# An FFT stage as two 64-row matmuls side by side, whole-row loads from SyncE, and a new order table

## The chip, the cores and the metric

The kernel runs on one core of one Trainium2 chip. The metric is the time of one launch on the device in microseconds (us), as the median of several launches on the same chip. One launch in each measurement is also recorded by the hardware profiler; the profile lines below come from that launch. A profile's span is 1.6 to 2.2 us shorter than the timed launch.

Names of the engines in the lines: PE is TensorE's matmul side, PEld its weight loads, DVE is VectorE, ACT is ScalarE, POOL is GpSimd, SP is SyncE (here it only issues loads and stores); a "q" behind a name (ACTq) is the engine's issuing side. L with a number is a line of the kernel.

## The reference

Four residual layers on x, 2048 x 640: a state-space recurrence A, a long convolution B gated by the normalized x, and both again with the same parameters.

```python
def _A_ref(x, Lambda_re, ..., Dskip):              # cut
    Lam_bar = exp(dt * Lam);  B_bar = ((Lam_bar - 1) / Lam)[:, None] * Bmat
    Bu = einsum("bld,pd->blp", x + 0j, B_bar)
    for t in range(L): h = Lam_bar * h + Bu[:, t]
    return 2 * einsum("blp,dp->bld", hseq, Cmat).real + x * Dskip

def _B_ref(q, k, v, shift_k, ssm_k, ssm_D):        # cut
    kv = causal_shift(k, shift_k) * v              # 4 taps
    y = irfft(rfft(pad(kv)) * rfft(pad(ssm_k)))[:S]
    return q * (y + kv * ssm_D)

x = x + _A_ref(_layernorm(x), ...)
x = x + _B_ref(_layernorm(x), B_k, B_v, ...)
x = x + _A_ref(_layernorm(x), ...)
x = x + _B_ref(_layernorm(x), B_k, B_v, ...)
```

The convolution does not depend on x. The kernel computes it once, in the "FFT part" up to some 160 us, beside the first pieces of layer A; the rest (the projections of the two A layers, chunk by chunk) is dense TensorE work.

## The kernel before

The 4096-point transforms are matmuls with small tables. Channels go through in five groups ("quarters"); each takes stage A (a table FA over 16 x 8 rows), an eviction from PSUM to SBUF, stage B (tables Cf, Sf), another eviction, products of spectra, and the inverse way. Stage A and the eviction helper:

```python
def evac(nc, eng, out, in_):                       # L285: one PSUM tile to SBUF, bf16
    if eng == "act":
        nc.scalar.activation(out, in_, ACT.Copy)
    else:
        nc.vector.tensor_copy(out, in_)

def stage_A(name, s_x, s_A, deps):
    outs = []
    for g in range(NOC // 4):                      # 4 tiles of 1024 f32 columns
        s_ps = R_ps.new()
        def e_m(_, g=g, s_ps=s_ps):
            pa = s_ps.get()[:].rearrange("p (o n) -> p o n", n=256)
            for o4 in range(4):
                nc.tensor.matmul(pa[:, o4, :], lhsT=s_x.get()[:, 4 * g + o4, :], rhs=T["FA"][:], start=True, stop=True)
        t_m = S.add(f"{name}:m{g}", "pe", c_mm(256, 4), deps + TK["fa"], e_m, uses=[s_ps, s_x, s_A])
        def e_e(eng, g=g, s_ps=s_ps):
            pa = ...                               # cut
            evac(nc, eng, vA(s_A.get())[:, :, 32 * g:32 * g + 32]..., pa)
        outs.append(S.add(f"{name}:e{g}", ("act", "dve"), ..., [t_m], e_e, uses=[s_A, s_ps]))
    return outs
```

PSUM is held by one ring of four tiles of 1024 columns, shared by all stages:

```python
"ps": store(psp, 4, "ps", [P, 1024], F32),
R_ps = St["R_ps"] = Ring(St["ps"], 4, lambda t: t[:], in_order=False)
```

Each `S.add` is a task with an engine (or two to choose from), an estimated time and its dependencies. A small scheduler, when the program is built, plays these estimates through and fixes every engine's order; the priorities come from a table of numbers per task name (`WHEN`). The engines then run their instructions strictly in that order. The two matrices B of layer A come in ten loads on ScalarE's queue, 256 B a row:

```python
for k in range(NJ):
    nc.scalar.dma_start(out=B[i][:, k], in_=src[:, k * P:(k + 1) * P].rearrange("(j p) e -> p j e", p=P))
```

The weights W0 and W1 come from C: 20 transposing loads, 20 scalings on ScalarE, 20 products on VectorE (two W per row block).

Of the kernel before, what the change touches and what calls it, by code (L numbers as in the profile page):

```python
# [9 lines left out]
ALU = mybir.AluOpType  # L10
# [7 lines left out]
P = 128  # L18
# [26 lines left out]
NB5 = 13  # L45
QGRP = [(0, 4), (4, 8), (8, 12), (12, 16), (16, 17)]
# [4 lines left out]
    "yt_io0": -271.6, "yt_ph0": 326, "yt_sin0": -120, "yt_neg0": -228.7, "yt_io6": 435.5, "yt_ph6": 22.8, "yt_sin6": -279.2, "yt_neg6": -141, "yt_io12":  # L51
    -220.6, "yt_ph12": -457.1, "yt_sin12": 437.4, "yt_neg12": 474.2, "yt_Ci": -245.6, "yt_Si": -161.3, "yt_nsi": -157.4, "yt_f0": -70.8, "yt_f1": -556.5,
    "yt_f2": -307.9, "yt_f3": -711.6, "yt_f4": 665.9, "kv_dsl": -59.1, "kv_d0": 150.8, "kv_d1": -77.1, "kv_d2": 0.9, "kv_ds0": -18.1, "kv_lk0": 528.3,
    "kv_lv0": 465, "kv_mm0": -259.3, "kv_ev0": -129.3, "kv_st0": -237.4, "kv_ds1": -220.1, "kv_lk1": -362.1, "kv_lv1": 704.6, "kv_mm1": 421.8, "kv_ev1":
    325.4, "kv_st1": 450.7, "kv_ds2": -305.2, "kv_lk2": 82.3, "kv_lv2": 465.6, "kv_mm2": -58.2, "kv_ev2": 145.9, "kv_st2": -165.8, "kv_ds3": 427.5,
    "kv_lk3": 70.5, "kv_lv3": 784.7, "kv_mm3": -40.1, "kv_ev3": 435.7, "kv_st3": -667.8, "kv_ds4": 512.6, "kv_lk4": -76.8, "kv_lv4": 422.1, "kv_mm4":
    -75.5, "kv_ev4": 132, "kv_st4": -45.9, "a_pl": -229.9, "a_p0": -261.5, "a_p1": 363.3, "a_p2": 347.9, "a_p3": -204.3, "a_p4": 255.2, "a_p5": 238,
    "a_p6": -249.8, "a_lamd": -396.5, "a_f": 2, "a_dd": -77.4, "a_ldB0": 23.4, "a_ldB1": -101.3, "a_wl00": -75.8, "a_wc00": -393.6, "a_wm00": -74.3,
    "a_wl01": 413.8, "a_wc01": -46.1, "a_wm01": 462.5, "a_wl02": 405.4, "a_wc02": -8.9, "a_wm02": -423.1, "a_wl03": 602.1, "a_wc03": 474.3, "a_wm03":
    -284.3, "a_wl04": 398.8, "a_wc04": -220.6, "a_wm04": -196.3, "a_wl10": -330.9, "a_wc10": -726.1, "a_wm10": 480.1, "a_wl11": 96.3, "a_wc11": -174.6,  # L60
    "a_wm11": -121.9, "a_wl12": 540.6, "a_wc12": 315.8, "a_wm12": 384.3, "a_wl13": -423.6, "a_wc13": 415, "a_wm13": -86.8, "a_wl14": 94.7, "a_wc14":
    -197.2, "a_wm14": -366.3, "a_b00": 339.9, "a_b0e0": -243.8, "a_b01": -303.4, "a_b0e1": -84.2, "a_b10": 367, "a_b1e0": 297.9, "a_b11": 537.4, "a_b1e1":
    -116.3, "a_gm0": -283, "a_ge0": 230.7, "a_gm1": 391.6, "a_ge1": 422.7, "a_gm2": 365.8, "a_ge2": -84.5, "a_gm3": 457.2, "a_ge3": 101, "a_gm4": 211.1,
    "a_ge4": -226.2, "a_t0": 91, "a_t1": -216.1, "a_t2": -113.7, "yq0_kl": -341.3, "yq0_ka": -222.8, "yq0_KA": 241, "yq0_KB": 409.1, "yq0_vl": -144.2,
    "yq0_VA": 324.9, "yq0_VB": -344, "yq1_kl": 361.5, "yq1_ka": -99.1, "yq1_KA": -347.4, "yq1_KB": -93.8, "yq0_pw": 251.1, "yq0_IB": -230.3, "yq0_tt":
    -225.5, "yq1_vl": 52.6, "yq1_VA": -147.3, "yq1_VB": -360.3, "yq0_IA": -427.3, "yq0_st": -247.4, "yq2_kl": -176.6, "yq2_ka": 326.8, "yq2_KA": -106.6,
    "yq2_KB": -222.6, "yq1_pw": -315.3, "yq1_IB": 346.7, "yq1_tt": -85.5, "yq2_vl": 505.1, "yq2_VA": 425.8, "yq2_VB": -57.5, "yq1_IA": 342.6, "yq1_st":
    -310.8, "yq3_kl": -681.2, "yq3_ka": -307.1, "yq3_KA": -687.6, "yq3_KB": 367.3, "yq2_pw": 540.8, "yq2_IB": -72.6, "yq2_tt": -46.2, "yq3_vl": 303.2,
    "yq3_VA": -299.1, "yq3_VB": -173.9, "yq2_IA": 544.4, "yq2_st": 512.3, "yq4_kl": -221.5, "yq4_ka": 583.5, "yq4_KA": 313.2, "yq4_KB": -706.1, "yq3_pw":
    75, "yq3_IB": -253.9, "yq3_tt": 477.5, "yq4_vl": -383.9, "yq4_VA": -63.8, "yq4_VB": 435.3, "yq3_IA": 285, "yq3_st": -339.1, "yq4_pw": 430.2, "yq4_IB":  # L70
    -600.2, "yq4_tt": -149.8, "yq4_IA": 302.1, "yq4_st": 393.8, "xl0": -445.4, "A1c0_ln_bn": 274, "A1c0_ln_sd": -264.9, "A1c0_ln_post": -71.3, "A1c0_id":
    -56.3, "A1c0_tu": -45.4, "A1c0_bp": 410, "A1c0_ev": -115.6, "A1c0_ri": -445.4, "A1c0_sc": -70.1, "A1c0_cy": -117.7, "A1c0_ro": -414.3, "A1c0_xr": 405,
    "A1c0_cp": -348.8, "A1c0_xe": -161.7, "xl1": 349.4, "A1c1_ln_bn": -263.7, "A1c1_ln_sd": 426.3, "A1c1_ln_post": -182.2, "A1c1_id": -45.6, "A1c1_tu":
    -390.5, "A1c1_bp": 554.8, "A1c1_ev": 433.4, "A1c1_ri": 62.5, "A1c1_sc": -176.6, "A1c1_cy": 692.2, "A1c1_ro": 257.4, "A1c1_xr": -229.1, "A1c1_cp":
    -301.2, "A1c1_xe": -187.2, "xl2": 489.2, "A1c2_ln_bn": 185.5, "A1c2_ln_sd": 42.9, "A1c2_ln_post": -273.1, "A1c2_id": -275.6, "A1c2_tu": 506.7,
    "A1c2_bp": 419.2, "A1c2_ev": -192.7, "A1c2_ri": -352.9, "A1c2_sc": 513.9, "A1c2_cy": 479.9, "A1c2_ro": 47.2, "A1c2_xr": 427.3, "A1c2_cp": 353.2,
    "A1c2_xe": -295.7, "xl3": 473.4, "A1c3_ln_bn": 436.7, "A1c3_ln_sd": -180.6, "A1c3_ln_post": -95.8, "A1c3_id": 501, "A1c3_tu": -171.8, "A1c3_bp":
    -284.2, "A1c3_ev": -23.6, "A1c3_ri": 474.8, "A1c3_sc": 262.9, "A1c3_ro": -55.3, "A1c3_xr": 88.2, "A1c3_cp": -259.4, "A1c3_xe": -282.6, "yl0": -306,
    "B1c0_ln_nm": -98, "B1c0_ln_sq": 59.3, "B1c0_ln_sd": 316, "B1c0_ln_post": 264.9, "B1c0_u": 256.2, "B1c0_m": 580.5, "A2c0_ln_nm": -307.9, "A2c0_ln_sq":
    -182.8, "A2c0_ln_sd": -188.6, "A2c0_ln_post": -48.1, "A2c0_id": 264.9, "A2c0_tu": 351.8, "A2c0_bp": -344.1, "A2c0_ev": -255.5, "A2c0_ri": -339.4,  # L80
    "A2c0_sc": 454.9, "A2c0_cy": 294.9, "A2c0_ro": -132.7, "A2c0_cp": -140.3, "A2c0_xe": 146.6, "yl1": 548, "B1c1_ln_nm": -62.5, "B1c1_ln_sq": 488,
    "B1c1_ln_sd": 544.9, "B1c1_ln_post": -353.5, "B1c1_u": -21.4, "B1c1_m": -58.3, "A2c1_ln_nm": 16.9, "A2c1_ln_sq": 550.5, "A2c1_ln_sd": -350.9,
    "A2c1_ln_post": -111.4, "A2c1_id": -172.3, "A2c1_tu": -255.8, "A2c1_bp": -229.7, "A2c1_ev": -110.4, "A2c1_ri": -95, "A2c1_sc": 249.4, "A2c1_cy":
    -412.5, "A2c1_ro": 473.1, "A2c1_cp": 453.6, "A2c1_xe": -412.8, "yl2": -87.5, "B1c2_ln_nm": 384.2, "B1c2_ln_sq": -409.3, "B1c2_ln_sd": 477.3,
    "B1c2_ln_post": 152.3, "B1c2_u": 497, "B1c2_m": 217.2, "A2c2_ln_nm": 338.6, "A2c2_ln_sq": 536.1, "A2c2_ln_sd": -93.8, "A2c2_ln_post": -401.5,
    "A2c2_id": 276.9, "A2c2_tu": -287.5, "A2c2_bp": -481.5, "A2c2_ev": 390.2, "A2c2_ri": 354.5, "A2c2_sc": -258.3, "A2c2_cy": 318.6, "A2c2_ro": 461.6,
    "A2c2_cp": 663.3, "A2c2_xe": -375.5, "yl3": 106.6, "B1c3_ln_nm": -193.4, "B1c3_ln_sq": 442, "B1c3_ln_sd": -114.2, "B1c3_ln_post": -416, "B1c3_u":
    523.6, "B1c3_m": -137.8, "A2c3_ln_nm": -203.6, "A2c3_ln_sq": 311.2, "A2c3_ln_sd": -189.5, "A2c3_ln_post": 529.5, "A2c3_id": -41.6, "A2c3_tu": -51.1,
    "A2c3_bp": -163.8, "A2c3_ev": -88.5, "A2c3_ri": 467.4, "A2c3_sc": -424.5, "A2c3_ro": 249, "A2c3_cp": 120.6, "A2c3_xe": 3.3, "B2c0_ln_nm": -65.3,
    "B2c0_ln_sq": -228.2, "B2c0_ln_sd": -207.9, "B2c0_ln_post": -254.7, "B2c0_u": -207.5, "B2c0_m": -58.2, "B2c0_st": 220.9, "B2c1_ln_nm": -628.9,  # L90
    "B2c1_ln_sq": -280, "B2c1_ln_sd": -119.4, "B2c1_ln_post": -430.8, "B2c1_u": -47.4, "B2c1_m": -25.8, "B2c1_st": 511.3, "B2c2_ln_nm": 494.3,
    "B2c2_ln_sq": -346.8, "B2c2_ln_sd": -142.4, "B2c2_ln_post": -421.9, "B2c2_u": 480.3, "B2c2_m": 70.7, "B2c2_st": 246.6, "B2c30_ln_nm": -252.7,
    "B2c30_ln_sq": -253.9, "B2c30_ln_sd": -542.9, "B2c30_ln_post": -437, "B2c30_u": -53, "B2c30_m": 535.7, "B2c31_ln_nm": -332.9, "B2c31_ln_sq": 450.9,
    "B2c31_ln_sd": 582.3, "B2c31_ln_post": -162.7, "B2c31_u": 169.1, "B2c31_m": 482.4, "B2c31_st": -150, "B2c32_ln_nm": 242.5, "B2c32_ln_sq": -75.7,
    "B2c32_ln_sd": -334.8, "B2c32_ln_post": -61.5, "B2c32_u": -209.4, "B2c32_m": 425.8, "B2c33_ln_nm": 520, "B2c33_ln_sq": 510.3, "B2c33_ln_sd": -286.2,
    "B2c33_ln_post": 91.1, "B2c33_u": -240.3, "B2c33_m": -214.5, "B2c33_st": -561.6,
}

# [178 lines left out]
def c_act(n):  # L277
    return 0.05 + 0.00083 * n
# [1084 lines left out]
```

## Time and profile before

| | before |
|---|---|
| time, median of 4 launches | 371.06 us (370.37 to 372.15) |
| span of the profile | 368.1 us |
| PE, VectorE, ScalarE busy | 329.2, 316.3, 258.2 us |
| first matmul of stage B | 31.6 us |
| PE idle by columns (prediction's formula): to stage B, middle, tail | 23.5, 14.9, 9.6 us |

Kept apart by shape, an eviction of 1024 columns lasts 1.04 us on ScalarE and 1.22 us on VectorE:

```profile
L287 ACT ACTIVATE b<-ps 128x1024 bf16<-128x1024 f32 x103 | 99.9, 1041 | 13.6 <-PE ps L666 11.0 <-PE ps L1042 1.2 <-PE ps L1069 0.9
...
L289 DVE CAST b<-ps 128x1024 bf16<-128x1024 f32 x18 | 21.7, 1220 | 11.0 <-PE ps L1042 5.8 <-PE ps L1069 5.0 <-PE ps L1146 0.2
```

Stage A makes 1024 columns with four matmuls in 0.44 us. The two longest waits of PE itself between 26 and 160 us in the kernel before (us in total, times, longest) name those evictions:

```profile
PE ps L1064 <- ACT b L287: 3.3, 5, 1.5
PE ps L1042 <- ACT b L287: 1.8, 6, 0.4
```

Here L1042 is stage A, L1064 stage B.

### The profile page before, as it was taken

The page shows a single profiled execution, that of the slowest core. Times are in us where ns is not written, and L with a number is a line of the kernel's source. Part 1 is how long each engine was busy: PE and PEld are TensorE (multiplying, and loading weights), DVE is VectorE, ACT ScalarE, POOL GpSimd, SP SyncE. Part 2 cuts the span into 40 slices and gives each one's busy share as a digit, 9 for nine tenths or more (in the row PEclk, how much of TensorE's full clock was granted, in tenths as well). Part 3 has the DMA queues.
Part 4 walks back from the last instruction along what each step waited for, and adds up shares of the span by engine and source line. Part 5 has one row for each costly group of instructions (what it writes and reads, how often), then busy time and mean ns, then how long its engine had stood idle before and what let it go on. Part 6 is the DMA issues. An engine that isn't in the chain of part 4 may idle for free.

```text
span 368.1 us, 7994 instructions
## 1 busy us (share of the span) xinstructions
PE 329.2 (89%) x3332; PEld 247.8 (67%) x3332; DVE 316.3 (86%) x483; ACT 258.2 (70%) x402; POOL 22.1 (6%) x54
## 2 busy tenths in 40 slices
PE   0259998999998899899999999999999999999990
PEld 0137777877877688788578577577587855865550
DVE  8666579699699799399998999977978999999996
ACT  0397689996879999993158859896677440813893
POOL 6035502000000000000000000000000000000000
PEclk9999999999999999999999999999999999999996
DMA  9983999999999975766044760453014005040042
GB/s 205 199 151 92 212 183 187 228 184 181 253 190 228 177 142 110 112 204 128 0 77 112 154 262 3 99 154 104 2 27 117 3 0 73 2 143 2 36 144 107
DMA packets 124510, 45.88 MB, mean 125 GB/s; under 512 B 118709, under 2 KB 118714, under 8 KB 124474
## 3 DMA queue, kind: packets, MB, share of 16 engines
q1 hardware_dynamic: 115152, 43.20, 53.2%
q10 hardware_dynamic: 9322, 2.18, 3.6%
q8 instruction: 26, 0.43, 0.5%
q14 instruction: 10, 0.08, 0.1%
HBM read 17.38 MB, written 7.86 MB: 69 GB/s over the span
## 4 chain that ended last, share of the span: by engine, by line
PE 70%; ACT 13%; DVE 9%; issue 3%; DMA 2%; POOL 1%; ACTq 1%; DVEq 0%; POOLq 0%
PE ps L752 32%; PE ps L663 10%; PE ps L666 10%; ACT b L287 8%; PE ps L1000 5%; PE ps L512 3%; PE ps L1042 2%; DMA b<-in_B_ssm_k_dram 2%; DVE bs L599 2%; PE ps L1145 1%; PE ps L1146 1%; PE ps L1064 1%; ACT b L458 1%; PE ps L1067 1%; POOL b L392 1%
## 5 line engine op out<-in xcount | busy, mean ns | idle before, releaser
L287 ACT ACTIVATE b<-ps 128x1024 bf16<-128x1024 f32 (+3 forms) x126 | 110.2, 956 | 17.4 <-PE ps L666 14.8
L752 PEld LDWEIGHTS <-b 128*128 128x128 bf16 x880 | 67.7, 98 | 48.3
L752 PE MATMUL ps<-W,b 128*128 128x128 bf16 (+1 forms) x640 | 95.9, 299 | 0.0
L663 PE MATMUL ps<-b,BT 128*128 128x256 bf16 x400 | 56.7, 273 | 0.6 <-ACT b L287 0.5
L666 PE MATMUL ps<-b,BT 128*128 128x256 bf16 x400 | 56.7, 273 | 0.0
L619 ACT ACTIVATE b<-b,nmr,rstd 128x640 bf16<-128x640 f32 (+1 forms) x51 | 44.0, 918 | 7.4 <-DVE nmr L586 7.3
L701 DVE TENSOR_TENSOR_SCAN b<-rtab,b 128x1290 bf16<-128x1290 f32 x16 | 44.6, 2832 | 0.2
L663 PEld LDWEIGHTS <-BT 128*128 128x128 bf16 x400 | 38.7, 98 | 5.2 <-issue 0.9
L666 PEld LDWEIGHTS <-BT 128*128 128x128 bf16 x400 | 39.1, 98 | 4.5
L574 ACT ACTIVATE junk<-b,nmean 128x640 bf16<-128x640 f32 x48 | 39.8, 828 | 1.5
L1064 PE MATMUL ps<-b,b 128*128 128x128 bf16 x170 | 35.1, 219 | 4.0 <-ACT b L287 3.3
L1067 PE MATMUL ps<-b,b 128*128 128x128 bf16 x170 | 35.3, 219 | 0.0
L289 DVE CAST b<-ps 128x1024 bf16<-128x1024 f32 (+1 forms) x23 | 23.5, 1045 | 13.1 <-PE ps L1069 7.1
L1069 PE MATMUL ps<-b,b 128*128 128x128 bf16 x150 | 32.8, 219 | 0.0
L1066 PE MATMUL ps<-b,b 128*128 128x128 bf16 x150 | 32.8, 219 | 0.0
L752 PE MATMUL ps<-G,b 128*128 128x512 bf16 (+1 forms) x160 | 27.0, 299 | 0.0
L760 ACT ACTIVATE b<-ps 128x640 f32<-128x640 f32 x16 | 11.2, 699 | 21.6 <-PE ps L752 21.5
L1042 PE MATMUL ps<-FA,b 128*128 128x256 bf16 x160 | 22.6, 285 | 3.3 <-ACT b L287 1.8
L569 ACT ACTIVATE nmean<-sums 128x4 f32<-128x4 f32 (+1 forms) x15 | 3.0, 203 | 29.0 <-DVE b L764 22.7
L1042 PEld LDWEIGHTS <-b 128*128 128x128 bf16 x160 | 15.8, 102 | 7.9 <-issue 3.9
L1145 PE MATMUL ps<-b,b 128*128 128x128 bf16 x160 | 18.4, 219 | 0.9 <-DVE b L1006 0.9
L1000 PE MATMUL ps<-b,fd 128*128 128x512 bf16 x80 | 18.4, 379 | 0.6 <-ACT b L287 0.6
(207 smaller groups left out, 573.3 us busy)
## 6 DMA issues: line engine op xcount, KB each, us to landing
b<-in_A_x_dram SPq DMA_DIRECT2D x8, 640.0 KB, 5.4
b<-ysd SPq DMA_DIRECT2D x8, 640.0 KB, 4.2
kvd<-b SPq DMA_DIRECT2D x5, 512.0 KB, 3.1
b<-kvd SPq DMA_DIRECT2D x5, 512.0 KB, 4.3
ysd<-b SPq DMA_DIRECT2D x5, 512.0 KB, 4.0
out_dram<-b SPq DMA_DIRECT2D x8, 320.0 KB, 2.2
b<-in_B_ssm_k_dram SPq DMA_DIRECT2D x4, 512.0 KB, 5.8
tab<-in_A_B_im_dram ACTq DMA_DIRECT2D x5, 160.0 KB, 4.2
```

Source lines behind the costliest of these rows:

```text
L287: nc.scalar.activation(out, in_, ACT.Copy)
L574: nc.scalar.activation(small.junk, src(q), ACT.Square, bias=st["nmean"][:, i:i + 1], scale=1.0, accum_out=st["ssq"][:, i:i + 1])
L619: nc.scalar.activation(dst, src, ACT.Identity, bias=st["nmr"][:, i:i + 1], scale=st["rstd"][:, i:i + 1])
L663: nc.tensor.matmul(pb[:, jj, c2, :], lhsT=aw["BT1"][:, c2, j, k, :], rhs=uT[:, k, 0:2, :].rearrange("p t i -> p (t i)"), start=(k == 0), s ...
L666: nc.tensor.matmul(pb[:, jj, c2, :], lhsT=aw["BT0"][:, c2, k, j * P:(j + 1) * P], rhs=uT[:, k, 2:4, :].rearrange("p t i -> p (t i)"), star ...
L701: nc.vector.tensor_tensor_scan(gv, rt, gv, 0.0, ALU.mult, ALU.add)
L752: nc.tensor.matmul(pc[:, o0:o1], lhsT=lh, rhs=rh, start=(n == 0), stop=(n == len(ops) - 1))
L1000: nc.tensor.matmul(pk[:, 512 * b:512 * (b + 1)], lhsT=s_ds.get()[:, l, :], rhs=kT[:, t0:t0 + 512], start=(l == 0), stop=(l == 3))
L1042: nc.tensor.matmul(pa[:, o4, :], lhsT=s_x.get()[:, 4 * g + o4, :], rhs=T["FA"][:], start=True, stop=True)
L1064: nc.tensor.matmul(ps[:, g, 0, :], lhsT=T["Cf"].get()[:, q, :], rhs=are, start=True, stop=single)
L1066: nc.tensor.matmul(ps[:, g, 0, :], lhsT=T["Sf"].get()[:, q, :], rhs=A[:, 2 * q + 1, :], start=False, stop=True)
L1067: nc.tensor.matmul(ps[:, g, 1, :], lhsT=T["NSf"].get()[:, q, :], rhs=are, start=True, stop=single)
```

## The change

The intent is to use the two halves of TensorE's rows at once in stage A, where each output needs only 64 of the 128 rows, and to start earlier. Stage A:

```diff
-            pa = s_ps.get()[:].rearrange("p (o n) -> p o n", n=256)
+            pa = s_ps.get()[:].rearrange("p (h s o e) -> p h o s e", h=2, o=4, e=4)
             for o4 in range(4):
-                nc.tensor.matmul(pa[:, o4, :], lhsT=s_x.get()[:, 4 * g + o4, :], rhs=T["FA"][:], start=True, stop=True)
+                for h in range(2):
+                    hs = slice(64 * h, 64 * (h + 1))
+                    nc.tensor.matmul(pa[:, h, o4, :], lhsT=s_x.get()[hs, 4 * g + o4, :],
+                                     rhs=T["FA"][hs, :].rearrange("p (s e) -> p s e", e=4), start=True, stop=True)
...
-    T["FA"] = wp.tile([P, 256], BF, tag="FA", name="FA")
+    T["FA"] = wp.tile([P, P], BF, tag="FA", name="FA")
```

The loads, in whole rows and on SyncE, and the scheduler's model of the queue:

```diff
-            for k in range(NJ):
-                nc.scalar.dma_start(out=B[i][:, k], in_=src[:, k * P:(k + 1) * P].rearrange("(j p) e -> p j e", p=P))
+            nc.sync.dma_start(out=B[i], in_=src.rearrange("(j p) e -> p j e", p=P))
...
-                    dma_free = max(dma_free, t.finish) + t.xt
-                    t.seen = dma_free + 1.6
+                    head, tail = self.DMA[t.est > 0.6]
+                    dma_free = max(dma_free, now + head) + t.xt
+                    t.finish = eng_free[eng] = max(t.finish, dma_free - 1.1)
+                    t.seen = dma_free + tail
```

Cut here, with the rest of the diff: every number of the table `WHEN`; many task estimates; the cosine table as sine of the absolute value (three ScalarE passes, half of VectorE's phases); the rotation table of layer A partly on ScalarE; ssm_D by a small load and a PE transpose; W1 made only after G; the last chunk's output in two VectorE passes per row group.

## The prediction

> **What bounds the kernel now.** I read the page's first two parts, then the work by stage, then the chain of waits, then the timeline of the first 32 us.
>
> ```profile
> PE 329.2 (89%) x3332; PEld 247.8 (67%) x3332; DVE 316.3 (86%) x483; ACT 258.2 (70%) x402; POOL 22.1 (6%) x54
> ...
> PE   0259998999998899899999999999999999999990
> ...
> DVE  8666579699699799399998999977978999999996
> ACT  0397689996879999993158859896677440813893
> ```
>
> TensorE (PE) is busy almost everywhere, except in the first three slices (9.2 us each) and the last. The work by stage (stretch, its length, then busy time of PE, weight load, VectorE, ScalarE, GpSimd) shows three regimes:
>
> ```profile
> 0.00:14.80 14.80, 0.00 (x0) 0.01 (x1) 13.10 (x50) 0.56 (x1) 5.76 (x19) 1.00 1.04 219
> 14.80:31.60 16.80, 11.05 (x72) 7.51 (x73) 9.13 (x25) 13.37 (x23) 3.54 (x4) 1.00 0.83 128
> ...
> 112.00:128.00 16.00, 13.15 (x154) 10.24 (x152) 13.22 (x34) 15.97 (x20) 0.00 (x0) 1.00 1.05 190
> ...
> 160.00:358.50 198.50, 198.47 (x1733) 141.43 (x1730) 184.99 (x255) 125.43 (x233) 0.00 (x0) 1.00 0.32 84
> 358.50:368.10 9.60, 0.00 (x0) 0.00 (x0) 6.22 (x14) 3.29 (x7) 0.00 (x0) 0.68 0.26 102
> ```
>
> From 160 to 358.5 us PE never rests. Before 14.8 us it does nothing, and in between it shares the work with a ScalarE that is full in places (15.97 of 16.00 us). Busy PE is not PE at its rate, so I also counted columns. The chain has this group:
>
> ```profile
> 201.64 15.23 PE ps L752 x118
> ```
>
> Its 118 matmuls stream 35,840 columns: 35,840/2.4 GHz = 14.93 us, plus 118 x 2.5 ns = 15.23 us. With that formula all 3,332 matmuls, 748,200 columns in the program's order, cost 311.8 + 8.3 = 320.1 us. The span is 368.1 us, so PE idles 48.0 us. **Where:** 9.6 us are the tail after the last matmul. At 31.57 us the first real FFT stage (stage B of the first quarter) starts; by then PE had done 35 matmuls of 128 columns (1.95 us), 16 of 512 (3.45), 16 of 256 (1.75) and small transposes (0.9), 8.0 us in all, so 23.5 us of the start were idle. The other 14.9 us are small waits up to 160 us.
>
> Why the start is so slow, from the timeline (start, duration, engine; "q" is the engine's issuing side):
>
> ```profile
> 5.73 7.14 ACTq L442 DMA_DIRECT2D tab<-in_A_B_im_dram  x5
> ...
> 14.24 1.28 ACT L845 ACT_TABLE_LOAD   x1 [14.24 <-DVE b L837]
> ...
> 16.89 1.72 ACTq L442 DMA_DIRECT2D G<-in_A_B_re_dram  x2
> ...
> 18.65 0.56 ACT L928 ACTIVATE b<-b 128x256 f32<-128x256 f32 x2 [1.35 <-issue]
> ...
> 20.35 0.42 DVE L932 TENSOR_TENSOR FA<-b 128x256 bf16<-128x256 f32 x1
> ...
> 23.21 1.04 PE L1042 MATMUL ps<-FA,b 128*128 128x256 bf16 x4 [0.83 <-DVE b L1091]
> ```
>
> ScalarE issues loads until 14.2 us, and again up to 18.6 us, while its phases have lain ready since 6.9 us. The sines, hence FA, hence stage A, all wait for a queue that is not even computing.
>
> **What the Trainium skill says.** "TensorE: Matmul & The Clock Gate", section "Wait — 56ns, not 53.3ns?", gives N/2.4 GHz plus about 2.5 ns for back-to-back matmuls; the group above agrees to the hundredth. "TensorEngine Tiling (Array Packing)", "Key Properties", says that row tiles work in parallel, but that a change of tiling mode drains the engine; no trace of before has row tiles, so neither is shown. "DMA: Bandwidth & Descriptors", "Specifications", puts line rate at 512 B or more per transfer; the old B loads are rows of 256 B, and the page counts 118,709 of 124,510 packets below 512 B (mostly transposes). The same page's "Issuing engines are not separate DMA queues" says that another issuer saves only sequencer time. Here that time is large: 7.14 us for one matrix.
>
> **The change, part by part.**
> *Stage A.* 160 matmuls of 256 columns cost 160 x 109.2 ns = 17.5 us. Now there are 320 of 128 columns, in pairs on rows 0-63 and 64-127. If a pair runs together it costs one stream of 55.8 ns. Can two weight loads keep up? The last FFT stage runs 32 load-and-matmul couples of 64 columns in 0.93 us, 29 ns each, so two need 58 ns: 160 x 58 ns = 9.3 us, a saving of 8.2 us. Against it stand drains. One matmul of 128 columns lasts 219 ns from start to modelled end against 56 ns between starts, so I estimate at most 0.16 us per switch. In the new order stage A forms 12 runs, so 24 switches, at most 3.9 us. I take 6 us net.
> *Start.* The two B matrices become two loads on SyncE (10 issues before), ssm_k goes there too, ssm_D comes by a small load and a PE transpose, and ScalarE begins with two small loads. Working along the new order with the durations of before: VectorE's first phase is ready near 3.5 us; three rather than two passes of about 0.9 us per table block (3 blocks) fill ScalarE from about 4 to 12.6 us, FA's sine among them near 9.5 us; two masks on GpSimd give FA near 11 us. FA is then not the limit: VectorE, in order, passes about 21 small column operations (3 us) and one product (1.2 us) before it adds kd, so stage A starts near 16.4 us, not 23.2. Then the parameters, now issued only near 14-16 us, hold VectorE until about 18.5 us, and the second shift product waits for its v (the seventh load; at the 219 GB/s of the first 14.8 us, 4.3 MB take 19 us). Stage B starts near 24.3 us. By then PE has done 45 x 56 ns, 32 x 216 ns, 1.1 and 0.9 us = 11.4 us, so 12.9 us are idle instead of 23.5: **10.5 us gained**.
> *Middle.* ScalarE gets some 5 us more (absolute value per block, ten short table rows), mostly early; VectorE loses about 4 us in the phases and 4 us in the rotation table. In the new order the first recurrence projections stand before the last two quarters' stage A (first after 93.8 us of PE work, last stage A at 118.9, both reckoned without concurrency), where before they came just after it (105.8 against 105.7): dense PE work lies beside ScalarE's evictions. The order is made anew with measured DMA queue times. I grant it 2.5 of the 14.9 us; this is judgement.
> *Tail.* In the last chunk two VectorE passes of 0.82 us, of which the first no longer needs the deviation, replace 0.49 + 0.82 us there and a 0.92 us ScalarE pass. Before, VectorE took 6.4 us from the last matmul to its last result. After, seven passes at 0.75 us between starts and two pairs of tiny ones give about 6.2. So 0.
>
> Sum: 371.4 - 10.5 - 6 - 2.5 = 352.4 us, say 352.5.
>
> **The rivals.**
> (a) *Row tiles do not overlap, or drains eat it.* Then the stage A saving is 0: about 358 us. For it: nothing in this trace shows overlap. Against: halves of the array, weights and result banks are separate.
> (b) *ScalarE takes over as the bound of the FFT part.* It is full from 112 to 128 and from 136 to 160 us, evictions do not shrink, and it gets more work. Then stage A's saving turns into PE waiting for PSUM, and only the start is kept: about 359 us. Against: its early queue work is gone, and VectorE may evict too.
> (c) *DMA bounds the start anyway.* The first loads already move 219 GB/s. Then stage B could start near 27 us and the gain be 7 or 8 us: about 355. Whole rows and fewer descriptors speak against it.
> (d) *The new order is much better than I grant.* With half of the 14.9 us gone and full overlap of stage A the time is near 345 us.
>
> **Range and chances.** (a) and (b) both lose some 6 us, (c) 3, (d) gains 7; they are partly independent, so 346 to 360 us holds it 8 times in 10. Even (a), (b) and (c) together leave the loss of queue work at the start, and 2% is 364 us. Faster by over 2%: 0.95; within: 0.04; slower: 0.01.
>
> **What would show it.** Stage A: pairs of starts a few ns apart, or a group of eight taking about 0.23 us in a run (0.44 before); if 0.44, (a). Start: sines from about 4 us, first stage A near 16.4 and first stage B near 24 us. Middle: the PE idle by column count between that and 160 us, 12 or so against 14.9, and whether the waits in it name ScalarE's evictions, (b), or a load, (c). Last regime: about 198 us unchanged if the same work lies there. Tail: 9.6 us as before. Wrong it would be above all if the new order starves PE in the middle: I have not followed the middle instruction by instruction.

## More of the kernel before

The page of the kernel before: busy times of the engines (share of the span, number of instructions), packets of the loads and stores, and the costliest ScalarE group (busy us, mean ns of one, idle before it):

```profile
PE 329.2 (89%) x3332; PEld 247.8 (67%) x3332; DVE 316.3 (86%) x483; ACT 258.2 (70%) x402; POOL 22.1 (6%) x54
...
DMA packets 124510, 45.88 MB, mean 125 GB/s; under 512 B 118709, under 2 KB 118714, under 8 KB 124474
...
L287 ACT ACTIVATE b<-ps 128x1024 bf16<-128x1024 f32 (+3 forms) x126 | 110.2, 956 | 17.4 <-PE ps L666 14.8
```

The last line is what the argument will come back to. Its mean mixes shapes.

## The result, and the profile after

| | before | after |
|---|---|---|
| time, median of 4 launches | 371.06 us | 360.80 us (360.28 to 361.70) |
| ratio after/before, 95% interval | | 0.9724 (0.9691 to 0.9756) |
| span of the profile | 368.1 us | 358.5 us |
| PE work by columns | 320.1 us | 311.6 us |
| PE idle to stage B, middle, tail | 23.5, 14.9, 9.6 | 14.9, 21.5, 10.5 us |

Ratios here are the mean time of one kernel's fast runs over that of the other's of the same rounds, so they are not quite the ratios of the medians. Where I compare two experiments that ran on different chips, I take the difference of their ratios to before times 371 us; 0.001 is 0.37 us. The interval of one ratio is usually 0.002 to 0.003 to each side, about 1 us.

The kernel is faster by 2.8%, but 8.3 us slower than predicted, just outside the range. The page after:

```profile
PE 324.3 (90%) x3467; PEld 242.3 (68%) x3493; DVE 321.8 (90%) x482; ACT 253.2 (71%) x399; POOL 24.4 (7%) x57
...
DMA packets 118711, 45.90 MB, mean 128 GB/s; under 512 B 111629, under 2 KB 112914, under 8 KB 118674
...
L296 ACT ACTIVATE b<-ps 128x1024 bf16<-128x1024 f32 (+3 forms) x121 | 105.9, 957 | 28.9 <-PE ps L687 22.2
```

The evictions of 1024 columns are as many as before (101 on ScalarE and 20 on VectorE for 103 and 18) and as long (1038 and 1214 ns). The start, from the timeline after (start, duration, engine, operation):

```profile
12.90 0.63 SPq L450 DMA_DIRECT2D tab<-in_A_B_re_dram  x1
...
12.96 5.89 PE L1064 MATMUL ps<-b,fd 128*128 128x512 bf16 x16 [0.65 <-POOL fd L1041]
...
18.78 0.84 PE L1109 MATMUL ps<-FA,b 64*128 64x128 bf16 x24
...
26.09 0.22 PE L1133 MATMUL ps<-b,b 128*128 128x128 bf16 x1
```

Two things are to be seen. In the third line, 24 of the new small matmuls take 0.84 us. Take off about 0.22 us from the last one's start to its modelled end, and they are 27 ns each, 55 ns a pair: the two halves do run at once. That leaves of rival (a) only the cost of the switches of tiling; it is not seen in this line, but beside it, and experiment 1 will show it. In the second line the first 16 shift products take 5.89 us: up to 17.6 us most of their starts are 427 ns apart, from there on 216. They lasted 3.62 us in before, where they came later. The first eleven thus ran at half the rate, although the clock column says 1.00 there. So stage A starts at 18.78 us and not at 16.4 as predicted, and stage B at 26.09 instead of 24.3.

Stretches of the timeline after (length, then busy time of PE, weight load, VectorE, ScalarE, GpSimd; then clock, share of the transfer engines, GB/s):

```profile
112.00:128.00 16.00, 13.59 (x178) 11.60 (x173) 12.38 (x24) 15.88 (x20) 0.00 (x0) 1.00 1.04 210
128.00:144.00 16.00, 14.03 (x208) 12.73 (x206) 13.04 (x21) 15.97 (x21) 0.00 (x0) 1.00 0.31 68
...
160.00:348.00 188.00, 186.89 (x1616) 131.57 (x1630) 177.68 (x250) 115.38 (x219) 0.00 (x0) 1.00 0.33 85
348.00:358.50 10.50, 0.00 (x0) 0.00 (x0) 7.22 (x14) 1.42 (x4) 0.00 (x0) 0.69 0.24 94
```

From 160 us on PE is full as before. The tail grew by 0.9 us. The middle is where the saved work went: 21.5 us of PE idle for 14.9. The waits of PE there, after:

```profile
PE ps L1109 <- ACT b L296: 2.4, 4, 0.9
PE ps L684 <- ACT b L296: 1.7, 3, 0.6
PE ps L1064 <- ACT b L296: 1.4, 3, 0.7
PE ps L1133 <- ACT b L296: 1.4, 3, 0.7
```

Stage A (L1109) now heads the list: it waits for a PSUM tile that ScalarE has not emptied yet. This looks like the prediction's rival (b), "ScalarE takes over". The experiments show that this reading is right in its name and wrong in its kind.

### The profile page after: what moved, and what is told of

It reads as the page before. It is cut to its first block, busy times and chain, and to the rows that moved or that the text cites.

```text
span 358.5 us, 8291 instructions
## 1 busy us (share of the span) xinstructions
PE 324.3 (90%) x3467; PEld 242.3 (68%) x3493; DVE 321.8 (90%) x482; ACT 253.2 (71%) x399; POOL 24.4 (7%) x57
## 4 chain that ended last, share of the span: by engine, by line
PE 62%; ACT 14%; DVE 11%; DMA 5%; issue 4%; POOL 2%; SPq 1%; ACTq 0%; DVEq 0%; POOLq 0%
PE ps L773 31%; PE ps L687 9%; PE ps L684 9%; ACT b L296 8%; PE ps L522 4%; PE ps L1064 4%; DMA b<-b 2%; DVE b L298 2%; ACT b L466 1%; DMA b<-in_A_C_im_dram 1%; DMA b<-in_A_C_re_dram 1%; SPq L462 1%; PE ps L1214 1%; DVE b L1070 1%; PE ps L1215 1%
## 5 line engine op out<-in xcount | busy, mean ns | idle before, releaser
L296 ACT ACTIVATE b<-ps 128x1024 bf16<-128x1024 f32 (+3 forms) x121 | 105.9, 957 | 28.9 <-PE ps L687 22.2
L773 PEld LDWEIGHTS <-b 128*128 128x128 bf16 x880 | 67.6, 98 | 48.2
L773 PE MATMUL ps<-W,b 128*128 128x512 bf16 (+1 forms) x632 | 95.4, 299 | 0.4
L640 ACT ACTIVATE b<-b,nmr,rstd 128x640 bf16<-128x640 f32 (+1 forms) x42 | 35.7, 916 | 2.8 <-DVE nmr L607 2.0
L298 DVE CAST b<-ps 128x1024 bf16<-128x1024 f32 (+2 forms) x28 | 28.0, 1024 | 4.7 <-PE ps L1138 2.3
L781 ACT ACTIVATE b<-ps 128x640 f32<-128x640 f32 x15 | 10.5, 701 | 26.4 <-PE ps L773 26.4
L773 PE MATMUL ps<-G,b 128*128 128x128 bf16 (+1 forms) x151 | 26.5, 295 | 0.5
L1064 PE MATMUL ps<-b,fd 128*128 128x512 bf16 x75 | 20.6, 415 | 2.8 <-ACT b L296 1.9
L470 DVE SCALAR_TENSOR_TENSOR W<-b,s_F 128x640 bf16<-128x640 bf16 x20 | 17.2, 880 | 3.7 <-ACT b L466 3.5
L466 ACT ACTIVATE b<-b,s_F 128x640 f32<-128x640 bf16 x20 | 16.5, 832 | 5.2 <-DMA b<-in_A_C_im_dram 4.0
```

What stands on the lines that cost most here:

```text
L640: nc.scalar.activation(dst, src, ACT.Identity, bias=st["nmr"][:, i:i + 1], scale=st["rstd"][:, i:i + 1])
L773: nc.tensor.matmul(pc[:, o0:o1], lhsT=lh, rhs=rh, start=(n == 0), stop=(n == len(ops) - 1))
L1064: nc.tensor.matmul(pk[:, 512 * b:512 * (b + 1)], lhsT=s_ds.get()[:, l, :], rhs=kT[:, t0:t0 + 512], start=(l == 0), stop=(l == 3))
```

## The experiments

Two theories stood at first. Theory S: ScalarE has too much work in the FFT part, so PE time saved there becomes waiting; take work off ScalarE and the row halves will pay. Its rivals: the transfers are the limit; or the new order lost what the halves gained. Eighteen kernels ran on the chip. One more, which let ScalarE evict only half of each tile, was not run: it would have read memory never written.

**1. The row halves undone, all else as after** (FA padded with zeros to full rows: correct, 8.9 us more PE work).

```diff
-    T["FA"] = wp.tile([P, P], BF, tag="FA", name="FA")
+    T["FA"] = wp.tile([P, 2 * P], BF, tag="FA", name="FA")      # zeros outside each half
...
-   lhsT=s_x.get()[hs, 4 * g + o4, :], rhs=T["FA"][hs, :]...
+   lhsT=s_x.get()[:, 4 * g + o4, :], rhs=T["FA"][:, P * h:P * (h + 1)]...
```

> The changed kernel with only stage A put back to full rows: 320 matmuls of 128 columns over all 128 rows, against a rhs padded with zeros. Same order, same evictions. PE work grows by 160 x 55.8 ns = 8.9 us. Theory 1 (the middle is bound by evictions or loads, so the saved PE time became waits): under 3 us slower, PE idle between stage B and 160 us shrinks from about 20 to about 13 us. Rival (PE bounds everywhere, and the new order is simply worse): 7 to 9 us slower.

Measured: 361.55 us, ratio 0.9742 (0.9714 to 0.9770), 0.7 us slower than after, and the intervals overlap. PE idle from 26 to 160 us is 13.0 us instead of 20.1. So 8.9 us of PE work taken away by the halves came back as about 7 us of idle PE in the middle. The halves, which give the change its first name, are worth 0.7 us, at most some 2.

**2. The row halves alone, in the kernel before.** The diff is the one of stage A above, with the matching eviction pattern.

> The kernel before with only stage A split into row halves, order and everything else kept. PE work falls by 8.2 us. Theory 1 (evictions or loads bound the middle): 0 to 3 us faster. Rival (PE bound): 7 to 8 us faster, near 363.

Measured: 374.41 us, ratio 1.0079 (1.0051 to 1.0106), slower, which neither expectation had. Stretches of this kernel about one stage A, from 68 us on:

```profile
68.00:70.00 2.00, 1.07 (x32) 0.84 (x31) 2.00 (x3) 2.00 (x4) 0.11 (x1) 1.00 0.73 247
70.00:72.00 2.00, 1.31 (x28) 0.88 (x27) 2.00 (x4) 2.00 (x4) 0.00 (x0) 0.99 1.15 216
72.00:74.00 2.00, 1.99 (x23) 1.79 (x18) 0.16 (x1) 1.79 (x2) 0.00 (x0) 0.50 1.15 216
```

In the stage (68 to 72 us) VectorE and ScalarE are busy without a break, 2.00 of 2.00 us, and PE only 1.07 and 1.31. Right after it the granted clock (the first of the last three numbers) is 0.50. From 120 to 131 us it averages 0.69; before has nothing below 1.00 in its stretches between 31 and 358 us. With 0.58 over the 4 us from 72 on, some 5 us of clock are gone. Here a PE that finished early and waited lost its full rate right afterwards; that the waiting is the cause is a reading of this order of events, not tested by itself.

**3. Plain loads in place of the transposing ones** for k, v and C (wrong result).

```diff
-   nc.sync.dma_start_transpose(out=kT[:, KPAD:KPAD + L], in_=B_k[0][:, kb * P:(kb + 1) * P])
+   nc.sync.dma_start(out=kT[:, KPAD:KPAD + L], in_=B_k[0]...[kb])      # same bytes, no transpose; so for v and C
```

> The changed kernel with the 30 transposing loads (k, v and the C matrices) replaced by plain loads of as many bytes; the result is wrong on purpose. SyncE's issue time for them falls from 1.2-5.9 us each to about 0.5 us. Rival (loads bound the middle): at least 5 us faster. Theory 1 in its form of evictions: at most 2 us faster, the waits still name ScalarE's evictions.

Measured: 357.37 us, 0.9630 (0.9611 to 0.9648), 3.5 us faster than after, between the two expectations. The transfers' share between 48 and 64 us falls from 1.07 to 0.70. They cost something, but not the 8 us that are missing.

**4. Forty small matmuls on PE at the very start**, to have its clock up by the first products.

```diff
+   for _w in range(40):
+       nc.tensor.matmul(s_p0.get()[:, 512:512 + P], lhsT=ident_bf, rhs=ident_bf, start=True, stop=True)
```

> The changed kernel with 40 dummy matmuls of 128 columns on PE ahead of its first instruction, into a PSUM region that nobody reads. If PE ran at half rate because it had been idle, the first 16 shift products take 3.6 us instead of 5.9. Where the start then decides the end: 2 us faster. Where ScalarE, VectorE or loads are the limit after 20 us: within 0.7 us of the changed kernel.

Measured: 360.12 us, 0.9707 (0.9670 to 0.9744): no difference that can be told. The stretches say why:

```profile
9.00:13.00 4.00, 2.27 (x17) 1.54 (x17) 3.79 (x17) 3.47 (x6) 2.94 (x6) 0.53 0.89 171
13.00:17.00 4.00, 3.78 (x11) 1.54 (x13) 3.67 (x13) 1.72 (x4) 0.95 (x1) 0.62 1.04 245
```

The clock came up and fell again to about half at 9 us, where PE waits for the first tables (busy 2.27 of 4 us). The shift products still took about 5 us. Now that a change of clock is in the record, the column shows it; in after the column's 1.00 before the first recorded change is not a measurement.

**5. Longer evictions on ScalarE, and 6. on VectorE.** After each eviction the same engine copies a part of the tile once more (78 copies of 128 columns on ScalarE, 22 of 512 on VectorE; the result stays right).

```diff
+   if eng == "act":      # e5; with "dve" and 0:32 in e9; likewise in the other two eviction helpers
+       evac(nc, eng, A[:, 0, 0:8, 16 * g:16 * (g + 1)], pa[:, 0, 0:8])
    evac(nc, eng, A[:, :, :, 16 * g:16 * (g + 1)], pa)
```

> The changed kernel in which ScalarE copies 128 columns a second time after 78 of its FFT evictions (same data, same result), some 0.2 us each, 15 us in all, spread over the FFT part. Theory 1 (evictions bound the FFT part, and there ScalarE): at least half of it shows, 8 us slower or more. Rival (loads, or the order's own waits, bound it): under 4 us.

Measured: 378.51 us, 1.0168 (1.0115 to 1.0221): 16.5 us for 21.3 us more ScalarE time, 0.8 us each us. About 5 us of it are again half-rate clock.

> The changed kernel in which VectorE copies 512 columns a second time after 22 of its FFT evictions, some 0.65 us each, 14 us in all. If VectorE shares the bound with ScalarE: 6 us slower or more. If ScalarE alone is the bound: under 4 us.

Measured: 368.32 us, 0.9916 (0.9885 to 0.9946): 7.1 us for 13.6 us more VectorE time, 0.5 each. Of these, some 3.4 us are half-rate clock as well (two stretches of 3.4 us in this trace); without the lost clock the two costs are about 0.5 and 0.3 us a us. So the evictions lie on the path that sets the end. I read it as theory S: ScalarE is full. That was too quick, since these copies do two things at once: they fill the engine, and they keep a PSUM tile longer.

**7. The old order table under the new program.**

```diff
-WHEN = { ... }        # the new numbers
+WHEN = { ... }        # the numbers of before for the tasks that both have
```

> The changed kernel with the priorities of the order table of before for the tasks that both have; everything else kept. If the new table was a gain in the middle, as the prediction granted: 3 us slower or more. If the new table is no better for this program than any other: within 3 us.

Measured: 415.56 us, 1.1180 (1.1146 to 1.1214). The table is a list of numbers that fits only the program for which it was searched, so this does not say what "the order" is worth by itself.

**8. The B matrices back on ScalarE's queue in ten pieces**, and the first ssm_k there too, all else as after.

> The changed kernel with the two B matrices loaded in ten pieces of 256-byte rows from ScalarE's queue again, and the first ssm_k load too; order otherwise kept. The prediction's start step says that this costs ScalarE some 14 us of issuing and so moves stage B back by 6 us or more: 5 to 8 us slower. If a middle bound by evictions absorbs the start: under 2 us.

Measured: 365.06 us, 0.9832 (0.9791 to 0.9874), 4.0 us slower than after, less than the 5 to 8 expected. About half of the gain at the start is thus where the loads are issued and in how many pieces. The timeline of this kernel has the ten pieces on ScalarE's issuing side:

```profile
1.40 4.11 ACTq L451 DMA_DIRECT2D W<-in_A_B_im_dram  x5
...
17.71 2.70 ACTq L451 DMA_DIRECT2D tab<-in_A_B_re_dram  x5
```

In after, one whole-row load on SyncE took 0.63 us to issue (the timeline above).

**9 to 12. ScalarE's C scalings moved to GpSimd**: in after, in after with full rows, in before, and in before with the row halves.

```diff
-   nc.scalar.activation(s_wr.get()[1], s_wr.get()[0][:, 1, :], ACT.Copy, scale=st["F6"][...])
+   nc.gpsimd.tensor_scalar(s_wr.get()[1], s_wr.get()[0][:, 1, :], st["F6"][...], None, ALU.mult)
```

> The changed kernel with the 20 scalings of the C matrices (0.83 us each on ScalarE, 16.5 us in all, between SBUF tiles) moved to the idle GpSimd; ScalarE's order is otherwise kept. Theory 1 (ScalarE bounds the FFT part): 6 to 12 us faster than the changed kernel, 349 to 355 us. Rival (loads or the order's waits): under 3 us.

> The same relief of ScalarE, with stage A in full rows (8.9 us more PE work). Theory 1: with ScalarE relieved PE counts again, so this is at least 2 us slower than the relieved kernel with row halves, where without relief the two differed by about 0.7. Rival: still under 1 us apart.

> The kernel before with the same 20 scalings moved to GpSimd. Theory 1: the FFT part of before is bound by ScalarE too, so 4 to 10 us faster than before. Rival: under 2 us.

> The kernel before with the scalings on GpSimd and stage A in row halves. Theory 1: now the halves pay, 2 us or more faster than the kernel before with the scalings alone. Rival: no gain, or a loss as without the relief (+0.8%).

Measured: 367.65, 368.12, 373.59 and 376.96 us; ratios 0.9915, 0.9927, 1.0090 and 1.0173. All are slower than the kernels that they come from, by 7.1, 6.9 (against full rows), 3.3 and, against the split alone, 3.5 us. The test had failed as a test: ScalarE lost its 16.5 us, and a slower step took their place. GpSimd's group and one wait of VectorE in the first of these kernels:

```profile
L466 POOL TENSOR_SCALAR b<-b,s_F 128x640 f32<-128x640 bf16 x20 | 39.4, 1975 | 84.9 <-DMA b<-in_A_C_im_dram 34.8 <-DVE b L298 20.2 <-DVE W L470 15.1
```

```profile
DVE W L470 <- POOL b L466: 8.4, 8, 2.2
```

GpSimd needs 1,975 ns for what ScalarE did in 832, and VectorE, which runs in order, waits for it 8.4 us. The halves are worth 0.4 us in this pair of after, and cost 3.1 in this pair of before.

**13 to 16. The scalings taken away, with nothing in their place** (VectorE reads the raw C; wrong result): in after, in after with full rows, in before, and in before with the row halves.

```diff
-   nc.scalar.activation(s_wr.get()[1], s_wr.get()[0][:, 1, :], ACT.Copy, scale=...)
...
-   ..., st["F6"][:, w, c, j:j + 1], s_wr.get()[1], ALU.mult, ALU.add)
+   ..., st["F6"][:, w, c, j:j + 1], s_wr.get()[0][:, 1, :], ALU.mult, ALU.add)
```

> Wrong result on purpose: the kernel after without the 20 scalings of C on ScalarE (832 ns each, 16.5 us); VectorE reads the raw C in their place, nothing else changes. Theory (ScalarE's evictions bound the FFT stages, so PE time saved in stage A turns into waits): the added ScalarE work of e5 cost some 0.6 us a us when the lost clock is taken off, so 16.5 us less should give 5 to 10 us: 351 to 356 us. Rival (the small waits of the middle come from the order and its chain of many different releasers, no engine in particular): at most 3 us, 358 or more.

> Wrong result on purpose: e14 with stage A in full rows again (8.9 us more PE work). Theory: with ScalarE relieved PE is nearer to being the bound, so the row halves now pay 2 to 5 us: e15 slower than e14 by that. Rival: as in e1 against after, 0.7 us, 1 at most.

> Wrong result on purpose: the kernel before without the same 20 scalings. Theory: before is bound by ScalarE in the middle as well (full from 112 to 128 us), with 14.9 us of PE idle there: 3 to 7 us faster, 364 to 368 us. Rival: under 2 us, since before's middle waits only 14.9 us in all and the order was made for it.

> Wrong result on purpose: e16 with stage A in row halves, the split alone. Theory: the split alone cost 0.8% in e2 because ScalarE could not follow and the clock dropped; relieved of 16.5 us, it should pay 1 to 4 us against e16. Rival (the split itself, by its switches of tiling mode or by a clock lost to short waits, costs time whatever ScalarE does): again 1 to 4 us slower than e16.

Measured: 357.46, 356.81, 369.66 and 372.59 us; ratios 0.9645 (0.9623 to 0.9668), 0.9613 (0.9589 to 0.9636), 0.9972 (0.9963 to 0.9981) and 1.0045 (1.0026 to 1.0064). Taking 16.5 us off ScalarE gives 2.9 us in after and 1.0 in before. The halves still do not pay: undone, the kernel is 1.2 us faster (within the intervals), and alone in before they cost 2.7 us, as the rival had it. Theory S fails in all four. PE idle from 26 to 160 us is 17.3 us with the halves and 9.1 without: again the 8.9 us of work return as idle time, now 8.2 us. The many executions of 15 and 16 also tell what the lost clock is worth. With a mean granted clock of 0.993 or more, the halves (five executions, 370.1 to 371.5 us) cost 1.3 us against nine of experiment 15 (369.0 to 370.0 us); with 0.981 or less (seven executions) they take 371.9 to 374.8 us. So about half of the 2.7 us goes with lost clock, and the rest does not.

**17. Transfers and ScalarE relieved together**: no scalings, plain loads, and the sines and fills of the rotation table, which stand where ScalarE is full (118 to 130 us), replaced by a constant. Its output is wrong, which doesn't matter for the time.

> Wrong result on purpose: after with three loads taken off at once. No C scalings (e14), plain loads for k, v and C (e3), and the rotation table's sines, absolute value and row fills, with their table loads some 7 to 8.5 us of ScalarE at 118 to 130 us, where ScalarE is full and e14 took nothing away, replaced by a constant that GpSimd writes. Theory J (transfers and ScalarE are the bound of the FFT part together, each alone only moves the wait to the other): more than the sum of e14 (2.8 us) and e3 (3.4) plus a part of the 8.5, so 10 to 15 us less than after: 346 to 351 us, and PE idle between 26 and 160 us down from 21.5 to under 10. Rival (many short waits of an order in which each engine runs in sequence; each relief gives its own small share): the sum at most, 6 us, 354 us or more, and PE idle still 15 us or more.

Measured: 354.74 us, 0.9551 (0.9538 to 0.9564), 6.4 us faster than after: the sum of 2.9 and 3.5, no more, and PE idle from 26 to 160 us is still some 15 us, as the rival had it. There is no joint bound. In this kernel ScalarE has 8.85 of 16 us busy from 112 to 128 us, and PE still idles 2 us there:

```profile
32.00:48.00 16.00, 15.46 (x282) 14.18 (x282) 15.48 (x18) 14.17 (x19) 6.27 (x27) 1.00 0.85 245
48.00:64.00 16.00, 14.12 (x160) 9.58 (x160) 15.55 (x16) 7.95 (x12) 1.32 (x2) 1.00 0.61 109
...
112.00:128.00 16.00, 14.57 (x187) 12.97 (x187) 12.35 (x31) 8.85 (x12) 1.82 (x2) 1.00 1.00 212
```

From 48 to 64 us VectorE (the third busy time) is full, and ScalarE half idle. So it was the last suspect.

**18. VectorE relieved as well**: the 20 products that make W and the two phase passes of the rotation table go from VectorE too; GpSimd writes a constant into W. Its output is wrong, which doesn't matter for the time.

> Wrong result on purpose: e19 with VectorE relieved as well. The 20 products that make W (0.88 us each) and the two phase passes of the rotation table (3.5 us) go from VectorE; GpSimd writes a constant into W. In e19, as in after, VectorE has almost no idle time from 26 to 64 us (before idled 5 to 10 us of it there), and of the removed work 8.6 us lie in that stretch. Theory V (VectorE is what bounds the FFT part after the earlier start, so relief elsewhere gave little): 5 to 9 us less than e19's 354.7, so 346 to 350 us, and PE idle between 26 and 64 us down from 7.1 to 3 or less. Rival (short waits of an order in sequence, no engine in particular): again a small share, 3 us at most, 352 us or more, with PE idle from 26 to 64 us at 5 or more.

Measured: 354.63 us, 0.9559 (0.9535 to 0.9583), no change against experiment 17. PE idle from 26 to 64 us fell from 7.1 to 5.1 us, but the time did not follow. A dip of the clock to 0.57 at 112 to 116 us took part of it: the two executions with a mean clock of 0.99 took 352.8 and 353.8 us, against 353.9 for the one of experiment 17 at 0.992. PE still idles 15 us between 26 and 160 us, some 1.7 of them by that dip; the rival's 5 us or more from 26 to 64 us came true too. From 64 to 80 us, where 3.1 us of that lie, all that ScalarE does is this group:

```profile
L296 ACT ACTIVATE b<-ps 128x1024 bf16<-128x1024 f32 (+2 forms) x18 | 16.0, 1012 | 0.5 <-PE ps L1102 0.4 <-PE ps L1208 0.2
```

These are evictions and nothing else, 16 us in 16 us.

**What these runs leave: the evictions themselves, and the switches of tiling.** The traces of three kernels, read at the same places, show both. First the evictions. The timeline of PE after, at stage A (L1109):

```profile
58.31 1.47 PE L1109 MATMUL ps<-FA,b 64*128 64x128 bf16 x32
60.26 1.02 PE L1064 MATMUL ps<-b,fd 128*128 128x512 bf16 x3 [0.49 <-ACT b L296]
...
65.66 1.05 PE L1109 MATMUL ps<-FA,b 64*128 64x128 bf16 x24
66.91 0.40 PE L1109 MATMUL ps<-FA,b 64*128 64x128 bf16 x8 [0.20 <-ACT b L296]
...
75.20 0.84 PE L1109 MATMUL ps<-FA,b 64*128 64x128 bf16 x24
76.77 0.40 PE L1109 MATMUL ps<-FA,b 64*128 64x128 bf16 x8 [0.73 <-ACT b L296]
```

The same stages with full rows, experiment 1:

```profile
58.01 1.99 PE L1110 MATMUL ps<-FA,b 128*128 128x128 bf16 x32
...
60.05 1.24 PE L1065 MATMUL ps<-b,fd 128*128 128x512 bf16 x4
...
65.35 1.95 PE L1110 MATMUL ps<-FA,b 128*128 128x128 bf16 x32
...
75.05 1.50 PE L1110 MATMUL ps<-FA,b 128*128 128x128 bf16 x24
76.83 0.61 PE L1110 MATMUL ps<-FA,b 128*128 128x128 bf16 x8 [0.28 <-ACT b L296]
```

And after with all the removable work of the three engines taken away, experiment 18:

```profile
64.32 1.05 PE L1102 MATMUL ps<-FA,b 64*128 64x128 bf16 x24
65.57 0.40 PE L1102 MATMUL ps<-FA,b 64*128 64x128 bf16 x8 [0.20 <-ACT b L296]
...
72.98 0.84 PE L1102 MATMUL ps<-FA,b 64*128 64x128 bf16 x24
74.55 0.40 PE L1102 MATMUL ps<-FA,b 64*128 64x128 bf16 x8 [0.73 <-ACT b L296]
```

A stage A fills four PSUM tiles of 1024 columns, which is the whole ring. In halves the 32 matmuls need 16 x 55 ns = 0.88 us. From the first of them to PE's next work after the run pass 1.95 us (58.31 to 60.26), with full rows 2.04 us (58.01 to 60.05): saved 0.09 us and not 0.87. In the next runs three tiles (x24) go at once, and the fourth (x8) waits 0.2 or 0.73 us for a tile that ScalarE is still emptying. Of stage A's 40 tiles ScalarE empties 27 and VectorE 13. Back to back, evictions start every 0.91 us on ScalarE and every 1.14 on VectorE, so the two together empty one tile every 0.5 us at best (an estimate from these two numbers), four in 2 us, however fast the matmuls are.

In experiment 18 the same two waits are there to the hundredth, 0.20 and 0.73 us: the work that was removed does not set them. That does not mean that VectorE is free. At the wait of 0.73 us it is busy in both kernels with products of spectra, which belong to the FFT. These lines are from after, VectorE and then ScalarE:

```profile
75.14 1.29 DVE L1195 TENSOR_TENSOR b<-b,b 128x2176 bf16<-128x2176 bf16 x1
76.35 1.22 DVE L1070 TENSOR_TENSOR b<-ps,b 128x1024 bf16<-128x1024 f32 x1
...
75.70 3.77 ACT L296 ACTIVATE b<-ps 128x1024 bf16<-128x1024 f32 x4 [1.23 <-PE ps L1109]
```

So ScalarE empties all four tiles of this stage alone (and those of the last one, at 142 us), and a shift product holds the fourth tile of the ring until VectorE reads it at 76.35. Which engine evicts which tile is fixed by the scheduler; another sharing was not tried.

Now the switches. Between 33 and 37 us there are four runs of stage A of one tile each (8 matmuls), and none waits for an eviction. The first in after, with the matmuls beside it:

```profile
33.39 0.22 PE L502 MATMUL ps<-b,tab 128*128 128x128 bf16 x1
33.54 0.40 PE L1109 MATMUL ps<-FA,b 64*128 64x128 bf16 x8
33.87 0.23 PE L501 MATMUL ps<-b,W 128*128 128x128 bf16 x1
```

The same in experiment 1:

```profile
33.14 0.22 PE L502 MATMUL ps<-b,tab 128*128 128x128 bf16 x1
33.20 0.61 PE L1110 MATMUL ps<-FA,b 128*128 128x128 bf16 x8
33.65 0.22 PE L501 MATMUL ps<-b,W 128*128 128x128 bf16 x1
```

With full rows every start follows the one before after 0.056 us. With halves 0.15 us pass from L502 to the first half, and again 0.15 us from the last pair to L501: a change of tiling costs about 0.095 us each way. The halves save 0.22 us on such a tile, and the two changes take 0.19 of it back. All twelve runs of stage A have at least these 0.095 us in front; behind them it stands alone in five and is otherwise part of a longer wait.

From first matmul to next work the twelve runs take 20.65 us in halves and 22.33 with full rows. Counted from the end of the work before, so that the first change is in it, they take 21.9 and 22.6 us (ends by the column formula): 0.7 us saved, where the columns say 8.9, and 0.7 us is also the difference of the two kernels. Of the 8.2 us lost, the changes that stand alone are at least 1.3; the rest is waiting for tiles. The pace of evictions also fits with longer evictions costing time, while less other work on ScalarE gave only 0.18 us a us (2.9 of 16.5).

The Trainium skill has a section for just this, "TensorEngine Tiling (Array Packing)", "PSUM Bottleneck": tiling speeds up TensorE but not the emptying of PSUM, which may become the bottleneck. The trace agrees, with 0.22 us a tile for the matmuls against 0.5 us for two evicting engines. The kernel already uses both engines, as the section advises, but not in every stage. I had read the page and cited another section.

What stays open: I could not make evictions shorter and keep the program defined, so the gain from a shorter eviction is not measured, only the loss from a longer one. Nor was a VectorE that evicts more of stage A's tiles tried. Why the halves alone in before are slower (2.9, 3.1 and 2.7 us in three pairs), and not just equal, is shown in part only: about half goes with lost clock (experiments 15 and 16), and the changes of tiling are there too, but what the other half is made of was not taken apart. No run beats after with a right result beyond the noise; full rows or warm-up (experiments 1 and 4) are within it. Relief of transfers and ScalarE would give 6.4 us, but those kernels compute something else.

## Why the prediction was wrong

Spans: before 368.1, after 358.5, so 9.6 us gained. Experiment 1 splits it, because its order is that of after and its PE work (311.6 + 8.9 = 320.5 us) is nearly that of before. Its span is 359.4 us, so PE idles 38.9 us: 14.8 at the start, 10.6 in the tail, 13.5 between.

| step of the prediction | predicted | measured | from |
|---|---|---|---|
| start | 10.5 | 8.6 | idle to stage B 23.5 and 14.9 us |
| **stage A** | **6** | **0.7 (0.9 in spans)** | experiment 1 against after |
| middle (order and all else) | 2.5 | 1.4 | 14.9 before, 13.5 in experiment 1 |
| tail | 0 | -0.9 | 9.6 and 10.5 us |
| sum | 19.0 | 9.8 to 10.0 | timed: 10.3 |

**The step that failed is "Stage A".** Its costs were right: the pair costs one stream (55 ns against the 55.8 to 58 reckoned), PE's work fell by 8.5 us, and the 2.2 us set aside for 24 switches fit what was measured (24 x 0.095 = 2.3 us, an upper estimate, since some of them hide in waits). What it took for granted is that the remaining 6 us of PE time in stage A are time of the kernel; 0.7 were, and the rest became waiting for PSUM tiles. I saw 0.44 us a tile in before and never set it against the 0.5 us that two engines need to empty one. In the order of after, most runs of stage A go at the pace of evictions even with full rows (experiment 1), so nothing below 0.44 could help there; in the four short runs it was the switches that took the gain. The prediction did hold the mechanism as rival (b), with the right outcome for this term ("only the start is kept: about 359 us"), but it argued from ScalarE's busy share and dismissed it because "VectorE may evict too". The count has to include both engines, as far as they are free at that moment, and it is made per tile, not per stretch.

**Start.** The mechanism was right (sines from 4 us, loads off ScalarE; experiment 8 gives 4.0 us for the queue and the pieces alone). The size was off by 1.9 us: I priced 32 shift products at 216 ns, and the first eleven came 427 ns apart, at a clock not yet up. Rival (c), loads as the bound of the start, has a part at most: plain loads (experiment 3) left stage B where it was, as the idle time up to 26 us (15.6 for 15.8 us) shows.

**Middle.** What is left for the order, 1.4 us, is close to the 2.5 granted. That is partly luck: it is the remainder of all the other changes together, and the 2.5 was called judgement. The column count between stage B and 160 us, which the prediction named as a test with "12 or so against 14.9", came out at 20 (21.5 with what lies after 160 us, as in the table above): the saved work is in it.

**Tail.** VectorE's passes of the last chunk take 0.88 us, 0.80 from start to start and not 0.75, and there are eight and not seven of them from the last matmul on.

**Chances.** "Faster by over 2%" was right at 2.8%. The range failed at its upper end because (b) and the mis-sized start came together with a tail that I had set to zero.

## What to carry to other kernels

Before a matmul is made faster, set its time per PSUM tile against the time in which all evicting engines together empty one; if the matmul is already the shorter, the saving turns into waiting. Ask also what the evicting engines do at that very moment, and how many matmuls stand between two changes of tiling: with 8 here, two changes of 0.095 us took back nearly all of 0.22. A busy share shows none of this, since an engine with idle time elsewhere still takes the same 1.04 us for the one tile that PE needs next. Undo one part of a bundle of changes with the order kept: here that one run (experiment 1) would have told at once which part had earned the gain.

## What the Trainium skill lacked or had wrong

- "TensorEngine Tiling (Array Packing)", "Key Properties": it says that a change of tiling mode drains the engine, but gives no cost. Here a change cost about 0.095 us each way: 0.15 us from start to start where full-row matmuls follow each other after 0.056.
- The same page, "PSUM Bottleneck": right, but it speaks of a 4-fold speedup and gives no number. Here the bottleneck is met already with full rows: 0.44 us a tile of matmuls against 0.5 us of eviction by two engines (a start every 0.91 and 1.14 us).
- "TensorE: Matmul & The Clock Gate", "What's actually happening": it gives the full rate after about 3.4 us of sustained work. Here 40 matmuls from 2.3 us on did not help, as the clock was back at 0.53 from 9 to 13 us; and in experiment 2 the clock fell to 0.50 after 4 us in which PE was busy 2.4 us, with no single wait above 0.93 us. The section speaks of an idle window of about 3.4 us. Further on the page does tell of a clock that goes up and down with short idles between groups of matmuls, but not at what busy share.
- "DMA: Bandwidth & Descriptors", "Issuing engines are not separate DMA queues": it calls the time of issuing usually small. Five pieces of one matrix took ScalarE 7.14 us in before, and moving ten such pieces and one more load back cost the kernel 4.0 us.
- No page that I read says that the profile's clock column shows 1.00 before the first recorded change: matmuls of 512 columns came 427 ns apart under it.
